# Attention and mixture-of-experts in one kernel: four new plans for the order of its steps

## The chip, the core and the metric

One NeuronCore of a Trainium2 chip runs the whole program, in one launch. The metric is the device time of that launch in microseconds (us), the median of several executions.

## What is computed

The reference pools k and v by 8 along the sequence, forms softmax attention of 8 batches with 8 heads, and sends the 4608 resulting tokens through a two-level mixture of 4 x 4 experts, where each token goes to one expert:

```
k_p, v_p = k, v averaged over 8 neighbours          # (8, 8, 72, 64)
attn     = softmax(q @ k_p.T / 8) ; attn_out = attn @ v_p
x        = attn_out as 4608 tokens of 512 numbers
g        = argmax(x @ w_group)  ; g_w = softmax weight of g
e        = argmax(x @ w_expert[g]) ; e_w = softmax weight of e
out      = g_w * e_w * (relu(x @ w1[g, e]) @ w2[g, e])
```

Everything is float32. The kernel makes the large products exact by splitting each operand into a rounded part and a rest and adding three products.

## The kernel before

The kernel works batch by batch. `Att` (L171) holds the attention and the router of one batch of 576 tokens, `Moe` (L570) the expert products of one batch, `Left` (L669) the tokens that did not choose their batch's most common expert. Three batches are in work at a time: while the expert products of batch b run, the attention of batch b+1 runs between them, and the inputs of batch b+2 are loaded and pooled.

Nothing is scheduled by a tool at run time. The order of the steps is four strings, START, FIRST, STEADY and LAST (L34 to L92), which `run` (L927) reads word by word: a word such as `n.nm:4:v` calls the method `nm` of the next batch's attention with the arguments 4 and "v". The letter ahead of the dot says whose step it is: `a` and `m` are attention and experts of batch b, `n` the attention of b+1, `w` the experts of b+1, `x` the attention of b+2, `l` the left-over tokens, `t` a warm-up or a small load. START runs once ahead of batch 0, FIRST is batch 0, STEADY is used for each of batches 1 to 6, LAST is batch 7. Each engine takes its instructions strictly in the order that these strings give it, and so do the DMA queues of SP and ACT; an instruction that waits holds up all that stand behind it on its engine.

The steps that the text speaks of, with their lines and engines:

- `kr`, `vr`, `rr` (L235, L253, L239) pool k, v and the 16 remaining rows. Their last argument picks the form: "p" three additions on Pool (L228, L229, L233), "v" the same three on DVE, "r" one reduction on DVE (L225).
- `sc`, `mx`, `sb`, `ex`, `su_`, `nm` (L328 to L376) are scores, maximum, subtraction, exponential, sum and division for one of 5 pieces of the sequence; `nm` multiplies on Pool ("p") or DVE ("v"), L373 and L376. `px_` and `pm` (L381, L400) turn the result on TensorE; `pxa`, `pma` (ACT) and `pxd`, `pmd` (DVE) split it. `av`, `ava`, `avd` (L418, L421, L425) multiply by v and split the result x.
- `kt` and `kta` (L287, L308): the pooled k turned on TensorE and taken out of PSUM by ACT. `sc` needs it.
- `xr` (L432): x put together again by eight additions on Pool; `rt` (L441) multiplies it by the router's weights, `route` (L455 to L483), `count` (L489), `main_expert`, `elect` (L496 to L508) find the batch's most common expert on DVE, and `gex`, `gates`, `keep_x` (L539 to L568) the gates.
- `w.load` (L584) loads the eight 512 KB weight slices of that expert over SP's queue, `split` (L591) rounds a slice on ACT, `spd` (L596) subtracts to get the rest, 2.4 us on Pool or 1.2 us on DVE.
- `up`, `ua`, `upd` (L609, L614, L619): first product on TensorE, relu on ACT, rest on DVE. `down`, `da` (L648, L661): second product and its output. Both use the same three PSUM buffers, so a product starts only when an earlier result was taken out.
- `l.step` (L692 to L757) builds the list of left-over tokens, `l.which` (L759) picks the first group, `l.xtiles` (L806) fills two 128 x 2304 tiles with zeros on Pool (L810).

Of the kernel before, what the change touches and what calls it, by code (L numbers as in the profile page):

```python
# [34 lines left out]
t.warm:20 a.load_v:0 a.vr:0:r a.load_k:1:w a.load_r:k a.load_k:0:w a.load_r:v t.warm:4 a.load_v:1 t.load_wr t.warm:18 a.load_q:0 a.kr:1:v a.load_q:4  # L35
a.rr:v a.kb a.load_q:1 t.warm:11 a.kr:0:p a.kt a.kta a.rcopy a.load_q:2 n.load_r:v a.vr:1:v a.guess_x a.qt:0 n.load_r:k a.guess_e a.qta:0 a.qt:1
a.qta:1 a.vmain m.load:1:1 a.sc:0 a.mx:0 a.vm:0 a.sb:0 a.ex:0 a.sc:1 a.su_:0 a.vm:1 n.load_k:1 t.warm:4 a.nm:0:v a.mx:1 a.px_:0 m.load:1:3 a.pm:0
a.pxa:0 a.vrem a.pma:0 m.load:1:2 a.sb:1 a.pxd:0 a.ex:1 a.vrx t.warm:7 a.pmd:0 t.warm:2 a.su_:1 a.av:1:0:128 a.av:0:0:128 a.ava:1:0:128 a.avd:1:0:128
a.load_q:3 a.ava:0:0:128 a.nm:1:p a.qt:2 m.load:1:0 a.avd:0:0:128 a.av:2:0:128 a.qta:2 a.av:3:0:128 a.ava:2:0:128 n.load_v:0 a.ava:3:0:128 n.load_k:0
a.avd:2:0:128 n.load_qb:0 a.sc:2 a.avd:3:0:128 n.load_qb:2 m.split:1:1 a.pm:1 a.px_:1 n.load_qb:3 a.mx:2 a.pxa:1 a.pma:1 a.sb:2 a.ex:2 m.split:1:0  # L40
m.spd:1:0:p a.pxd:1 a.qt:3 a.qta:3 a.pmd:1 t.warm:8 a.av:1:128:128 a.ava:1:128:128 a.su_:2 a.av:2:128:128 a.av:3:128:128 m.spd:1:1:p a.avd:1:128:128
n.load_qb:1 a.av:0:128:128 a.ava:2:128:128 a.ava:0:128:128 a.avd:0:128:128 a.ava:3:128:128 a.avd:3:128:128 a.sc:3 a.avd:2:128:128 m.up:0:0 m.ua:0:0
# [3 lines left out]
a.pma:2 a.mx:4 a.su_:3 m.spd:1:2:v t.warm:4 a.sb:4 m.up:4:0 m.split:1:3 a.nm:3:p a.ex:4 a.pxd:2 a.pmd:2 a.su_:4 n.vr:0 m.up:2:0 m.ua:4:0 a.pm:3
m.upd:4:0 a.nm:4:p a.px_:3 m.ua:2:0 m.upd:2:0 a.pma:3 a.pxa:3 a.px_:4 a.pxa:4 a.pmd:3 a.pxd:3 m.up:3:0 a.pm:4 a.pma:4 m.upd:1:0 a.pxd:4 a.pmd:4
m.ua:3:0 a.av:2:256:320 a.ava:2:256:320 a.avd:2:256:320 m.split:2:0 n.kr:0:r a.av:0:256:320 a.ava:0:256:320 m.upd:3:0 a.av:1:256:320 a.av:3:256:320
m.load:2:2 a.ava:3:256:320 a.ava:1:256:320 m.spd:1:3:p n.kr:1:p a.avd:3:256:320 m.up:5:0 n.rr:p m.split:2:1 m.ua:5:0 m.spd:2:1:p a.avd:1:256:320
m.spd:2:0:p a.avd:0:256:320 n.load_v:1 m.up:6:0 m.ua:6:0 m.upd:5:0 a.rt n.kt n.kta m.upd:6:0 n.qb:0 m.up:1:1 n.qb:1 a.route n.sc:0 n.mx:0 n.sb:0  # L50
n.ex:0 m.up:7:0 a.count x.load_r:v n.sc:1 m.ua:7:0 n.qb:2 n.su_:0 m.up:0:1 n.rcopy n.nm:0:p n.mx:1 m.upd:7:0 n.px_:0 m.ua:0:1 m.ua:1:1 m.up:2:1 n.sb:1
n.ex:1 m.upd:0:1 n.qb:3 x.load_k:1 n.su_:1 n.nm:1:p a.gex n.sc:2 n.pxa:0 n.mx:2 n.vrem m.upd:1:1 m.load:2:3 m.ua:2:1 m.up:4:1 n.pm:0 m.upd:2:1 n.px_:1
x.load_r:k m.ua:4:1 n.pxa:1 m.up:3:1 n.pm:1 n.sb:2 n.pxd:0 n.pma:1 m.ua:3:1 a.keep_x n.qb:4 n.vr:1:p t.warm:4 t.warm:2 n.vmain a.gates n.ex:2
# [919 lines left out]
```

## Time and profile before

| | us |
|---|---|
| three executions | 599.0, 599.31, 601.17 |
| their median | 599.31 |
| the profiled execution, on its own clock | 602.23 |
| its span, first to last instruction | 600.4 |
| TensorE busy | 573.5 |
| DVE busy | 408.2 |
| Pool busy | 303.9 |
| ACT busy | 277.6 |

The profile is one execution. In the views below a line starts with the time of its first instruction in us from the span's start and its length; in brackets stand the idle time ahead of it and what ended that. The mean granted clock of TensorE was 0.98 of full speed. Two levels are seen, 1.00 and 0.50.

### The profile page before, as it was taken

The page shows a single profiled execution, that of the slowest core. Times are in us where ns is not written, and L with a number is a line of the kernel's source. Part 1 is how long each engine was busy: PE and PEld are TensorE (multiplying, and loading weights), DVE is VectorE, ACT ScalarE, POOL GpSimd, SP SyncE. Part 2 cuts the span into 40 slices and gives each one's busy share as a digit, 9 for nine tenths or more (in the row PEclk, how much of TensorE's full clock was granted, in tenths as well). Part 3 has the DMA queues.
Part 4 walks back from the last instruction along what each step waited for, and adds up shares of the span by engine and source line. Part 5 has one row for each costly group of instructions (what it writes and reads, how often), then busy time and mean ns, then how long its engine had stood idle before and what let it go on. Part 6 is the DMA issues. An engine that isn't in the chain of part 4 may idle for free. (4 is left out here: it accounts for less than half of the span.)

```text
span 600.4 us, 13256 instructions
## 1 busy us (share of the span) xinstructions
PE 573.5 (96%) x4970; PEld 511.4 (85%) x4970; DVE 408.2 (68%) x1104; ACT 277.6 (46%) x621; POOL 303.9 (51%) x296
## 2 busy tenths in 40 slices
...
DMA packets 119362, 81.45 MB, mean 136 GB/s; under 512 B 76790, under 2 KB 95990, under 8 KB 118912
## 3 DMA queue, kind: packets, MB, share of 16 engines
...
## 5 line engine op out<-in xcount | busy, mean ns | idle before, releaser
L609 PE MATMUL mm<-xt,w 128*128 128x320 f32 (+1 forms) x1536 | 225.8, 302 | 7.4 <-DVE kT L755 4.7
L609 PEld LDWEIGHTS mm<-xt,w 128*128 128x128 f32 x1536 | 209.7, 191 | 11.3 <-DVE kT L755 4.9
L648 PE MATMUL mm<-w,ht 128*128 128x512 f32 x744 | 184.7, 400 | 0.0
L596 POOL TENSOR_TENSOR w<-sw,w 128x1024 fp32r<-128x1024 f32 x55 | 131.6, 2401 | 82.5 <-ACT w L591 69.2
L648 PEld LDWEIGHTS mm<-w,ht 128*128 128x128 f32 x744 | 139.0, 191 | 30.2 <-issue 1.8
L614 ACT ACTIVATE ht<-mm 128x320 fp32r<-128x320 f32 (+1 forms) x128 | 52.2, 410 | 76.1 <-PE mm L609 73.9
L619 DVE SCALAR_TENSOR_TENSOR ht<-mm,ht 128x256 fp32r<-128x256 f32 (+1 forms) x192 | 63.9, 367 | 28.1 <-ACT ht L614 27.7
L591 ACT CAST w<-sw 128x1024 fp32r<-128x1024 f32 x64 | 67.0, 1047 | 31.7 <-DMA sw<-in_moe_w_dram 28.4
L432 POOL TENSOR_TENSOR sw<-xt 128x256 f32<-128x256 f32 (+1 forms) x56 | 43.6, 807 | 46.9 <-DVE xt L425 46.9
L661 ACT ACTIVATE y<-mm,gm 128x512 f32<-128x512 f32 x31 | 21.3, 687 | 89.6 <-PE mm L648 88.2
L342 DVE TENSOR_REDUCE mx<-sc 128x8 f32<-128x576 f32 (+1 forms) x40 | 30.0, 751 | 41.3 <-PE sc L336 40.6
L373 POOL TENSOR_TENSOR px<-p,su 128x128 f32<-128x128 f32 (+1 forms) x38 | 17.1, 450 | 72.0 <-DVE su L365 58.1
L376 POOL TENSOR_TENSOR p<-p,su 128x576 f32<-128x576 f32 (+1 forms) x38 | 43.8, 1152 | 3.0
L358 ACT ACTIVATE p<-p 128x576 f32<-128x576 f32 (+1 forms) x40 | 27.4, 685 | 24.4 <-DVE p L353 19.9
L425 DVE TENSOR_TENSOR xt<-tp,xt 128x320 fp32r<-128x320 f32 (+2 forms) x68 | 28.8, 439 | 12.4 <-ACT xt L421 11.2
L336 PEld LDWEIGHTS sc<-kT,qT 64*64 64x64 f32 x1264 | 24.2, 137 | 14.2 <-issue 8.1
L363 DVE TENSOR_REDUCE su<-p 128x8 f32<-128x576 f32 (+1 forms) x40 | 29.9, 747 | 8.8 <-ACT p L358 8.7
L336 PE MATMUL sc<-kT,qT 64*64 64x72 f32 x1264 | 30.2, 234 | 5.2 <-ACT kT L308 2.0
L421 ACT CAST xt<-tp 128x320 fp32r<-128x320 f32 (+2 forms) x68 | 25.4, 387 | 18.8 <-PE tp L418 16.7
L653 PE MATMUL mm<-w,ht 128*128 128x512 f32 x128 | 31.8, 392 | 0.0
L353 DVE TENSOR_TENSOR p<-sc,mx 128x288 f32<-128x288 f32 x70 | 28.6, 450 | 2.8 <-POOL rp L273 0.7
L653 PEld LDWEIGHTS mm<-w,ht 128*128 128x128 f32 x128 | 24.0, 188 | 5.7 <-issue 0.6
(235 smaller groups left out, 757.4 us busy)
## 6 DMA issues: line engine op xcount, KB each, us to landing
...
```

Of the source, the lines that this page charges most:

```text
L336: nc.tensor.matmul(ps[t:t + 64, y, SP * g:SP * g + SP], lhsT=s.qT[c][r, g, t:t + 64], rhs=k, start=True, stop=True)
L342: red(out=mx[0:n], in_=scv, axis=AX.X, op=ALU.max)
L363: red(out=su[0:n], in_=s.p[c][0:n], axis=AX.X, op=ALU.add)
L376: eng.tensor_tensor(out=p[0:n], in0=p[0:n], in1=su[0:n].unsqueeze(3).broadcast_to([n, 2, 4, SP]), op=ALU.mult)
L432: nc.gpsimd.tensor_tensor(out=s.xw[g][:, sl], in0=s.xt[:, 0, g, sl].bitcast(F32), in1=s.xt[:, 1, g, sl].bitcast(F32), op=ALU.add)
L591: nc.scalar.copy(out=wh, in_=raw)
L596: (nc.vector if eng == "v" else nc.gpsimd).tensor_tensor(out=wl, in0=raw, in1=wh.bitcast(F32), op=ALU.subtract)
L609: nc.tensor.matmul(ps[:, 0:n], lhsT=l[:, kc, fs], rhs=xt[:, r, kc, sl], start=(kc == 0 and i == 0), stop=(kc == 3 and i == 2))
L614: nc.scalar.activation(out=s.ht[f][:, o:o + n], in_=s.pu[f, hf][:, 0:n], func=AF.Relu)
L619: stt(out=ht[:, at:at + hi - lo], in0=ps[:, lo - o:hi - o], scalar=0.0, in1=ht[:, lo:hi].bitcast(F32), op0=ALU.max, op1=ALU.subtract)
L648: nc.tensor.matmul(ps, lhsT=s.ht[f][:, 640 * l + o:640 * l + o + 128], rhs=s.w[2, f // 2][r][:, f % 2, :], start=(i == 0), stop=(i == 23))
L653: nc.tensor.matmul(ps, lhsT=s.ht[f][:, 512:640], rhs=s.w[2, f // 2][r][:, f % 2, :], start=(i == 0), stop=(i == 15))
```

## The change

Only the four strings are different; no function is touched, and START has one line more, so that every line number of the program is one higher. The same steps are called with the same data. What is different is their order on every engine, the number of warm-up matmuls (87 calls instead of 95), and for some steps the engine. The words that a reader needs, of some 110 changed lines:

```
 FIRST = """
-x.load_qb:2 n.av:1:0:256 n.nm:3:p n.px_:3 n.pxd:2 n.pxa:3 n.ava:1:0:256 n.mx:4 n.sb:4 n.ex:4 t.warm:1 m.spd:2:2:p x.load_qb:0 n.pxd:3 n.su_:4 n.pm:3
-n.pma:3 m.down:0 m.down:1 m.split:2:3 n.av:0:0:256 n.pmd:3 n.av:2:0:256 n.ava:0:0:256 n.nm:4:v n.avd:1:0:256 n.avd:0:0:256 n.av:3:0:256 n.ava:2:0:256
+m.upd:4:1 n.pmd:2 n.pxa:2 n.av:1:0:256 n.nm:3:p n.mx:4 n.px_:3 n.sb:4 n.ava:1:0:256 n.ex:4 n.pxd:2 n.su_:4 n.pxa:3 x.load_qb:1 n.avd:1:0:256 m.down:0
+x.load_v:0 n.nm:4:p n.pxd:3 n.pm:3 n.pma:3 m.down:1 m.split:2:3 n.pmd:3 n.av:0:0:256 m.spd:2:3:p n.ava:0:0:256 n.av:2:0:256 m.upd:7:1 n.av:3:0:256
...
 STEADY = """
-x.load_v:1 n.xr:3:256:320 m.down:0 x.kr:1:p m.down:1 x.kr:0:p n.rt m.down:2 m.da:0 m.down:6 m.down:3 n.route n.main_expert m.down:4 m.down:5 x.qb:0
-w.load:1:0 w.load:1:1 m.da:1 w.split:1:0 x.rr:v x.kt x.vr:1:v w.load:1:3 n.gex m.down:7 m.down:8 w.load:1:2 m.down:12 w.spd:1:0:p x.rcopy w.load:2:0
-x.vrem w.split:1:1 m.da:2 n.keep_x m.down:9 x.kta x.vmain w.load:2:1 x.sc:0 x.mx:0 x.sb:0 x.qb:1 n.gates x.ex:0 x.vm:0 m.down:10 m.down:13 x.su_:0
+n.av:2:0:256 n.avd:0:0:256 n.ava:2:0:256 x.kr:1:p x.load_r:k m.ua:7:1 n.xr:0:0:256 n.avd:1:0:256 n.avd:2:0:256 n.av:3:0:256 n.av:0:256:320
...
+n.avd:3:256:320 n.xr:2:256:320 n.xr:3:256:320 x.kr:0:r x.load_v:1 n.rt m.down:2 m.down:3 m.da:0 m.down:6 n.route x.qb:0 n.main_expert x.rr:r
+w.load:1:0 m.down:4 w.load:1:1 m.down:7 x.vr:1:p m.down:5 m.da:1 x.kt x.rcopy n.gex x.kta n.gates w.split:1:0 w.split:1:1 x.vrem m.down:8 w.load:2:0
+m.down:9 x.vmain w.spd:1:0:v x.sc:0 w.load:1:2 m.da:2 w.load:1:3 m.down:10 x.qb:1 x.vrx w.spd:1:1:p x.mx:0 x.sb:0 m.down:11 x.ex:0 m.down:12 m.da:3
...
 LAST = """
-l.xtiles m.upd:3:0 m.up:3:1 m.split:2:1 m.load:2:2 m.ua:4:1 l.which l.tiles m.spd:2:1:p m.upd:4:1 m.ua:3:1 m.up:5:0 m.upd:3:1 m.ua:5:0 l.fetch_x
+m.up:5:1 m.load:2:2 m.upd:3:0 l.xtiles m.split:2:1 m.upd:3:1 l.tiles m.spd:2:0:p m.up:5:0 m.ua:5:0 m.up:6:1 m.load:2:3 m.ua:5:1 m.split:2:2 l.which
```

Three places show what this does to the engines' queues. The first is ACT in STEADY, from the first outputs of batch b's second product (y) to the pooled k of batch b+2 (kT); w and sw are weight slices. Before:

```order
L661 ACTIVATE y<-mm,gm 128x512
L662 DMA out_dram<-y 128x512
L591 CAST w<-sw 128x1024
L539 ACTIVATE dg<-dg 128x20
L539 ACTIVATE de<-de 128x20
L247 DMA rp<-rp 32x128 x2
L272 CAST rh<-rp 32x128
L591 CAST w<-sw 128x1024
L661 ACTIVATE y<-mm,gm 128x512
L662 DMA out_dram<-y 128x512
L308 ACTIVATE kT<-tp 128x2x128
L309 ACTIVATE kT<-tp 128x2x16
```

And with the change:

```order
L662 ACTIVATE y<-mm,gm 128x512
L663 DMA out_dram<-y 128x512
L248 DMA rp<-rp 32x128 x2
L540 ACTIVATE dg<-dg 128x20
L540 ACTIVATE de<-de 128x20
L309 ACTIVATE kT<-tp 128x2x128
L310 ACTIVATE kT<-tp 128x2x16
L592 CAST w<-sw 128x1024 x2
L273 CAST rh<-rp 32x128
L261 CAST kp<-vp 128x256
L662 ACTIVATE y<-mm,gm 128x512
L663 DMA out_dram<-y 128x512
```

The two steps of `kta` stood behind both roundings of weight slices; now they stand ahead of them.

The second place is Pool in STEADY, around the eight additions of `xr` (sw from xt; kv, kp, vp are the pooling of k and v). Before:

```order
L373 TENSOR_TENSOR px<-p,su 128x128
L376 TENSOR_TENSOR p<-p,su 128x576
L432 TENSOR_TENSOR sw<-xt 128x256 x2
L432 TENSOR_TENSOR sw<-xt 128x320
L432 TENSOR_TENSOR sw<-xt 128x256 x2
L432 TENSOR_TENSOR sw<-xt 128x320 x3
L228 TENSOR_TENSOR kv<-kv 128x2x256
L229 TENSOR_TENSOR kv<-kv 128x2x128
L233 TENSOR_TENSOR kp<-kv 128x128
```

And with the change:

```order
L374 TENSOR_TENSOR px<-p,su 128x128
L377 TENSOR_TENSOR p<-p,su 128x576
L229 TENSOR_TENSOR kv<-kv 128x2x256
L230 TENSOR_TENSOR kv<-kv 128x2x128
L234 TENSOR_TENSOR vp<-kv 128x128
L229 TENSOR_TENSOR kv<-kv 128x2x256
L230 TENSOR_TENSOR kv<-kv 128x2x128
L234 TENSOR_TENSOR kp<-kv 128x128
L433 TENSOR_TENSOR sw<-xt 128x256 x4
L433 TENSOR_TENSOR sw<-xt 128x320 x4
```

Two poolings, of a half of v and a half of k, now run on Pool ahead of the eight additions; before, a pooling of k followed them (a second one stood behind it), and the half of v was DVE's.

The third place is DVE in LAST, where the list of left-over tokens is closed (kv, pos, kT, niti) and the first group picked (kb); ht is the rest of a first product. Before:

```order
L745 SCALAR_TENSOR_TENSOR kv<-kv,loh 128x640
L746 TENSOR_REDUCE pos<-kv 128x40
L747 TENSOR_SCALAR pos<-pos 128x40
L619 SCALAR_TENSOR_TENSOR ht<-mm,ht 128x256
L753 MEMSET it 128x1
L755 TENSOR_SCALAR kT<-cum 128x1
L756 CAST niti<-kT 128x1
L619 SCALAR_TENSOR_TENSOR ht<-mm,ht 128x256
L763 TENSOR_SCALAR kb<-cum,it 128x128
```

And with the change:

```order
L746 SCALAR_TENSOR_TENSOR kv<-kv,loh 128x640
L747 TENSOR_REDUCE pos<-kv 128x40
L748 TENSOR_SCALAR pos<-pos 128x40
L620 SCALAR_TENSOR_TENSOR ht<-mm,ht 128x256
L754 MEMSET it 128x1
L756 TENSOR_SCALAR kT<-cum 128x1
L757 CAST niti<-kT 128x1
L620 SCALAR_TENSOR_TENSOR ht<-mm,ht 128x256
L620 SCALAR_TENSOR_TENSOR ht<-mm,ht 128x64
L620 SCALAR_TENSOR_TENSOR ht<-mm,ht 128x256 x2
L620 SCALAR_TENSOR_TENSOR ht<-mm,ht 128x64
L764 TENSOR_SCALAR kb<-cum,it 128x128
```

The closing operations kept their order; the picking of the first group moved behind four more rests. On Pool, in both, a weight subtraction, the two fills of zeros and another subtraction follow one another there.

## Rows read from the trace of the kernel before

**Rows 1.** The page: busy time, share of the span and instructions of each engine.

```profile
PE 573.5 (96%) x4970; PEld 511.4 (85%) x4970; DVE 408.2 (68%) x1104; ACT 277.6 (46%) x621; POOL 303.9 (51%) x296
```

**Rows 2.** Waits of TensorE: engine, line, releaser: us in total, times, longest.

```profile
PE mm L609 <- DVE kT L755: 4.7, 1, 4.7
PE tp L418 <- DVE xt L425: 2.3, 1, 2.3
PE tp L489 <- DVE oh L483: 2.1, 2, 1.1
PE sc L336 <- ACT kT L308: 2.0, 1, 2.0
PE mm L609 <- ACT y L661: 1.8, 3, 1.2
PE sc L336 <- DVE p L349: 1.8, 1, 1.8
PE sc L336 <- DVE p L353: 1.2, 1, 1.2
```

**Rows 3.** TensorE in time: the router's product of batches 2, 3 and 7.

```profile
169.74 1.28 PE L441 MATMUL tp<-sw,wr 128*32 128x160 f32 x32
...
234.59 1.28 PE L441 MATMUL tp<-sw,wr 128*32 128x160 f32 x32
...
499.74 1.28 PE L441 MATMUL tp<-sw,wr 128*32 128x160 f32 x32
```

**Rows 4.** ACT in time, around 318 us (STEADY).

```profile
317.81 1.05 ACT L591 CAST w<-sw 128x1024 fp32r<-128x1024 f32 x1 [3.56 <-DMA sw<-in_moe_w_dram]
```

**Rows 5.** Pool, DVE and ACT in time, around 455 us (STEADY).

```profile
455.36 2.40 POOL L596 TENSOR_TENSOR w<-sw,w 128x1024 fp32r<-128x1024 f32 x1
...
455.46 2.31 DVE L549 SCALAR_TENSOR_TENSOR se<-sg,se 128x5 f32<-128x5 f32 x1
...
460.45 0.72 ACT L666 ACTIVATE y<-y,gm 64x512 f32<-64x512 f32 x1 [3.19 <-DVE y L665]
```

**Rows 6.** Pool and DVE in time, around 95 us (FIRST).

```profile
94.05 2.38 POOL L596 TENSOR_TENSOR w<-sw,w 128x1024 fp32r<-128x1024 f32 x1 [1.62 <-ACT w L591]
...
94.42 2.15 DVE L373 TENSOR_TENSOR px<-p,su 128x128 f32<-128x128 f32 x1
```

**Rows 7.** Two stretches behind it: length, PE, PEld, DVE, ACT, POOL busy, PEclk, DMA.

```profile
99.00:100.00 1.00, 1.00 (x4) 0.81 (x3) 0.84 (x4) 0.79 (x4) 0.70 (x2) 0.50 0.00 0
102.00:103.00 1.00, 1.00 (x7) 0.91 (x6) 0.26 (x1) 0.00 (x0) 0.00 (x0) 0.79 0.00 0
```

**Rows 8.** Pool, DVE and TensorE in time, around 540 us (LAST).

```profile
537.11 2.39 POOL L596 TENSOR_TENSOR w<-sw,w 128x1024 fp32r<-128x1024 f32 x1 [10.05 <-PE mm L609]
...
541.39 2.02 POOL L810 MEMSET pl<- 128x2304 f32 x1
...
537.37 6.08 DVE L747 TENSOR_SCALAR pos<-pos 128x40 f32<-128x40 f32 x1
...
524.26 14.60 PE L609 MATMUL mm<-xt,w 128*128 128x256 f32 x108
543.53 11.14 PE L609 MATMUL mm<-xt,w 128*128 128x320 f32 x60 [4.66 <-DVE kT L755]
```

**Rows 9.** Pool in time, around `xr` of batch 3 (STEADY).

```profile
228.28 0.74 POOL L432 TENSOR_TENSOR sw<-xt 128x256 f32<-128x256 f32 x1 [6.55 <-DVE xt L425]
...
234.88 1.30 POOL L228 TENSOR_TENSOR kv<-kv 128x512 f32<-128x512 f32 x1
236.26 0.74 POOL L229 TENSOR_TENSOR kv<-kv 128x256 f32<-128x256 f32 x1
237.08 0.50 POOL L233 TENSOR_TENSOR kp<-kv 128x128 f32<-128x128 f32 x1
```

**Rows 10.** DVE: its wait for the router's product, and a pooling as one reduction.

```profile
DVE lg L459 <- PE tp L441: 24.7, 7, 3.6
...
L225 DVE TENSOR_REDUCE kp<-kv 128x128 f32<-128x1024 f32 x1 | 2.0, 2031 | 0.0
```

More of the change, by code (lines that the diff above doesn't have):

```diff
@@ L34 @@
 START = """
[L35 to L42, printed above, removed]
+t.warm:21 t.load_wr a.load_k:0:w a.load_v:0 a.load_k:1:w a.load_r:k t.warm:18 a.load_r:v a.load_v:1 a.kr:0:v a.vr:0:r t.warm:4 t.warm:10 a.load_q:0
@@ new lines @@
+a.rr:v a.load_q:1 a.kr:1:p a.kb a.kt a.kta a.vr:1:v a.rcopy n.load_r:v a.load_q:2 a.guess_x a.qt:0 n.load_r:k a.guess_e a.vmain a.qt:1 a.vrem a.qta:0
+a.qta:1 a.sc:0 a.sc:1 a.mx:0 t.warm:4 a.vm:0 a.sb:0 a.ex:0 a.su_:0 n.load_k:1 a.vm:1 m.load:1:1 a.nm:0:p a.px_:0 a.load_q:3 a.vrx m.load:1:3
+m.load:1:2 a.qt:2 a.pxa:0 a.pm:0 a.mx:1 a.sb:1 a.pma:0 t.warm:7 a.pxd:0 a.ex:1 a.pmd:0 a.av:1:0:128 a.av:0:0:128 a.su_:1 a.qta:2 a.ava:1:0:128
+a.ava:0:0:128 a.avd:1:0:128 a.av:2:0:128 a.ava:2:0:128 m.load:1:0 a.nm:1:p a.av:3:0:128 a.ava:3:0:128 a.avd:0:0:128 a.load_q:4 n.load_k:0 a.sc:2
@@ L46 @@
[L46 to L53, printed above, removed]
@@ L62 @@
-x.kta m.down:9 m.down:7 x.sc:0 w.split:1:0 w.load:1:2 x.qb:1 x.mx:0 x.sb:0 w.load:1:3 x.vrem x.ex:0 w.load:1:1 w.load:2:1 m.down:8 n.gates x.su_:0
-w.spd:1:0:v m.da:2 w.split:1:1 x.nm:0:p m.down:12 x.vr:1:p m.down:13 m.da:4 x.vr:0:p m.down:10 m.down:11 m.da:3 w.spd:1:1:p x.vmain x.vm:1 w.load:2:0
-x.vrx n.keep_x x.vm:0
+m.ua:0:0 m.up:1:0 m.load:2:1 a.nm:2:p a.qt:4 m.ua:1:0 a.mx:3 a.sb:3 t.warm:2 m.upd:0:0 a.ex:3 a.pm:2 a.qta:4 a.px_:2 a.su_:3 a.sc:4 n.vr:0 a.mx:4
+t.warm:7 m.split:1:2 m.spd:1:2:v a.pma:2 m.up:4:0 a.nm:3:p a.sb:4 a.pxa:2 a.ex:4 m.up:2:0 a.pmd:2 a.pm:3 m.ua:4:0 a.px_:3 a.su_:4 m.ua:2:0 m.up:3:0
@@ new lines @@
+n.xr:0:0:256 n.pma:4 n.xr:3:0:256 n.pmd:4 n.av:0:256:320 n.av:1:256:320 x.kr:0:r n.ava:0:256:320 n.ava:1:256:320 n.avd:0:256:320 n.av:3:256:320
+n.avd:1:256:320 n.av:2:256:320 n.xr:0:256:320 n.ava:3:256:320 n.avd:3:256:320 n.xr:1:256:320 n.ava:2:256:320 m.down:3 n.xr:3:256:320 x.qb:0
+n.avd:2:256:320 n.xr:2:256:320 x.rr:r m.da:0 m.upd:6:1 m.down:4 n.rt x.kr:1:p m.down:5 n.route x.kt m.down:6 n.main_expert x.qb:1 m.da:1 m.down:7
+x.kta n.gex x.rcopy x.sc:0 x.mx:0 w.load:1:0 m.down:12 x.vrem x.sb:0 w.split:1:0 w.load:1:3 x.vrx x.ex:0 x.su_:0 m.down:8 w.spd:1:0:v w.load:1:1
```

61 lines of the change are left out of this document (35 added, 26 removed).

## The prediction, made before the change was run
> **What bounds the kernel now.** I read the page's busy times first, then TensorE's list of waits, then the five places that this list names, in order of time on all engines. The busy times show one engine that is hardly ever free: TensorE works 573.5 of 600.4 us [rows 1], so 26.9 us is all that any new order can win from gaps, and DVE, ACT and Pool matter only where TensorE waits for them. The list of waits says where: 4.7 us in LAST behind DVE's L755; in FIRST 2.3 us behind DVE's L425, 2.1 us behind L483 and 1.2 us behind L353; in STEADY 2.0 us behind ACT's L308 and 1.8 us behind ACT's L661; in START 1.8 us behind L349 [rows 2]. They add up to 15.9 us; the rest of the idle time is the launch, the end, and pieces of some tenths.
>
> What stands behind these waits is to be seen on two engines. In FIRST, Pool begins a weight subtraction of 2.38 us at 94.05, and DVE's small L373, which begins at 94.42, takes 2.15 us: it ends about when Pool's does [rows 6]. In STEADY, L549, five numbers per partition, takes 2.31 us beside a Pool operation of 2.40 [rows 5], and ACT then waits 3.19 us for DVE's y. In LAST, L747 takes 6.08 us beside a Pool queue of 2.39 us and two fills of 2.02 us each [rows 8]. So a small DVE operation between two SBUF tiles that comes just behind a Pool operation stands until Pool is done, and all of DVE's queue behind it: the evictions that free PSUM too. The wait for L308 is of another kind: ACT stood 3.56 us at a weight slice that had not landed [rows 4], with the eviction of kT queued behind it.
>
> A gap also costs afterwards. Behind the gap of 2.3 us in FIRST the granted clock is 0.50 from 99 on and 0.79 in 102 to 103 [rows 7], the lower of the two levels (1.2 and 2.4 GHz) for some 3.8 us, in which TensorE does what 1.9 us do at full clock. In LAST the 108 matmuls ahead of the gap took 14.60 us, 0.135 each; the 60 behind it took 11.14 where that rate gives 8.1, so 3.0 us more [rows 8].
>
> **The change, part by part.** TensorE's products are the same; eight of 95 warm-up calls go, but these stand where TensorE waits anyway, so I give them no term.
>
> FIRST: `nm` of piece 4 goes from DVE to Pool. L373 is then on Pool's own queue and cannot stand against it, and the evictions behind it (L425) come on time: 2.3 us of gap and 1.9 us of clock. The router's steps meet less Pool work, because the poolings of k stand elsewhere: the 2.1 us and 1.2 us can go. Ends: 0 and -7.5 us. I take -5, since the first 4.2 us have one clear cause and the other 3.3 us depend on Pool's new order.
>
> STEADY: the five intervals between the router's products of batches 2 and 7 last 499.74 - 169.74 = 330.0 us, the shortest 234.59 - 169.74 = 64.85 [rows 3]. Had all been like it, they would have taken 324.25: 5.75 us is lost to unlucky batches. The new order puts `kta` ahead of both roundings, so a late slice no longer holds the eviction of kT; and `gates` goes ahead of `sc` of the next batch, and with it L549 ahead of that Pool subtraction. Ends: 0 and -5.75; I take -5, because both named causes are gone by position. Three operations are added to DVE or changed there. `kr:0` and `rr` become reductions of 2.03 us [rows 10], the first where DVE waits 24.7 / 7 = 3.5 us per batch for the router's product [rows 10], the second behind `main_expert`, with no one waiting but the copy of rp; if that cover went, a batch would pay up to 2 us. The weight subtraction that goes to DVE stands in the same idle stretch. Loads on SP keep their number; k:0 goes ahead of the second slices, which wait for buffers anyway. The two poolings put on Pool ahead of `xr` take 2 x (1.30 + 0.74 + 0.50) = 5.1 us; Pool stood idle there for 6.55 us [rows 9], so they cost nothing with 1.5 us to spare.
>
> LAST: 7.7 us hang on L747 (4.7 of gap, 3.0 of clock). The order of the closing operations stays, and on Pool subtraction, fill, fill, subtraction still follow one another. The subtraction waits for the rounding of slice 1:3 (1.05 us, as in rows 4), the rounding for the relu of the same product whose rest DVE takes just ahead of L755. So the same matmul releases both, DVE has to bring its small operation through in about 1 us, and it has three operations of the list to finish first. Before, it missed by 0.26 us (537.37 against 537.11) [rows 8]. L747 itself stands two places earlier than L755 and should get through; L755 may well be caught. The Trainium skill, "SBUF — State Buffer", section "Who interferes with whom", says that the shared port pair is an exclusive lock for one whole instruction, and that the second to come waits until the first is finished; by that a caught L755 would go on after Pool's 2.4 us, before TensorE needs the buffer behind it, and the whole 7.7 us would be won. The row speaks against that here: L747 was not let in between the subtraction and the fills, but only after all three. By the row a caught L755 stands some 6 us, TensorE meets a full PSUM about 3 us later, and with the clock 5 to 6 of the 7.7 us come back. The picking of the first group (L763) then stands beside the next subtractions and can cost 1 to 2 us more. Ends: 0 and -7.7; I take -2, by the nearest row, L747.
>
> START: `nm:0` goes from DVE to Pool, a `kr` and `vr` change places. The four weight slices that end this stretch are asked for by the same chain, so I take 0; the ends are its one wait, 1.8 us, either way.
>
> New waits: hand-written places that are moved get gaps of their own; of the kind of L489, about 1.0 us each [rows 2]. I take two, +2 us; ends 0 and +4.
>
> Sum: -5 - 5 - 2 + 0 + 2 = -10 us. The profiled execution took 602.23, so 592.2. It lies 2.9 us above the median of the runs shown, 599.31; part of that may be the late slice at 318, if other executions do not have it, and the new order would not feel it. So I set no part of the 2.9 against the sum: **592 us**, 7 us below the median.
>
> **Rivals.**
> 1. The lock is handed over between Pool instructions, or L755 comes in time, and LAST gives all 7.7 us: 592.2 - 5.7 = 586.5 us. For it: DVE stood beside one Pool operation alone in its 2.31 us [rows 5]. Against it: the 6.08 us of L747 [rows 8]. It is what the page of the Trainium skill named above states as its rule.
> 2. Nothing is won in sum. The small operations are as many as before (DVE loses only the extra steps of pooling), every Pool operation is still there, and what is taken from one neighbour gets another: five waits of some 2 us come back elsewhere, about 599 us. For it: the best interval has no slack to give. Against it: the two STEADY causes vanish by order alone.
> 3. Slower. Pool's additions for `xr` now wait for a half of k that SP loads late in the batch, behind the q pieces, on the only engine that `rt` waits for. The cover is 1.5 us of Pool time. If the load, or `nm:4` ahead of it, is 4 us late, each of six STEADY batches loses 2.5 us at `rt`: 592 + 15 = 607 us. It decides from 1.7 us beyond the cover on, where 6 x 1.7 eats the 10 us. For it: DVE waits behind `rt`, and Pool's last addition ends within tenths of it. Against it: SP issues that load behind twelve of the sixteen q pieces, not at the end, and it needs no buffer that Pool has yet to free.
>
> **How the numbers follow.** Forecast 0.45, rival 1 0.22, rival 2 0.20, rival 3 0.13. A measurement of this kernel can tell 0.5%, 3.0 us, from no change, so "same" is 596.3 to 602.3. Forecast, rival 1 and a little of rival 2 lie below: faster 0.68. Most of rival 2: same 0.20. Rival 3: slower 0.12. The range goes from 584, which leaves out the case in which every end comes at its best (602.2 - 7.5 - 5.75 - 7.7 = 581.3), up to 601, which leaves out rival 3.
>
> **What would show it.** Right: TensorE's list of waits has no L308 and no L661 above a few tenths, the five intervals between router products all lie near 65 us, and in FIRST no gap of 2 us is left behind L425. L549 takes a fraction of a microsecond in most batches. In LAST, the length of L755 (L756 in the new numbering) tells forecast from rival 1: 2 us or less, or 4 to 6 us with a gap on TensorE behind it. Wrong: a wait of `rt` (L441, L442 in the new numbering) for Pool in every batch is rival 3; new waits of 2 us at names that the list does not have now are rival 2.

## Result and profile after

The changed kernel takes **578.14 us** (median of 4 runs, 577.8 to 578.97) against 599.61 in the runs beside it: a ratio of 0.964, 95% interval 0.9619 to 0.9662. The forecast was 592.0, the range 584 to 601. The direction was right; the gain is 21.5 us where 7 against the median were forecast, and the time lies 6 us below the range. (Line numbers after are one higher than before, L756 is what L755 was.)

The page's busy times of the change, then the head of TensorE's list of waits (us in total, times, longest):

```profile
PE 562.8 (98%) x4954; PEld 504.6 (88%) x4954; DVE 392.1 (68%) x1072; ACT 273.9 (48%) x621; POOL 305.8 (53%) x304
```
```profile
PE sc L337 <- DVE p L350: 1.7, 1, 1.7
PE mm L922 <- DVE valid L127: 1.1, 1, 1.1
PE tp L419 <- ACT ph L406: 0.7, 1, 0.7
```

Of [rows 2] only the wait in START is left at its size. TensorE's idle time went from 26.9 to 13.7 us. But its busy time fell as well, by 10.7 us [rows 1], with the same products and eight warm-up calls fewer: a part of what it was "busy" with was waiting, too. The mean granted clock of TensorE rose from 0.980 to 0.992; of the two levels 1.00 and 0.50 that is, as an estimate, some 24 us at the lower one before and 9 after.

The router's product of batches 2, 3 and 7 in time (answers to [rows 3]):

```profile
160.40 1.28 PE L442 MATMUL tp<-sw,wr 128*32 128x160 f32 x32
...
225.01 1.28 PE L442 MATMUL tp<-sw,wr 128*32 128x160 f32 x32
...
483.47 1.28 PE L442 MATMUL tp<-sw,wr 128*32 128x160 f32 x32
```

Read as stages, these products and the spans say where the time came from:

| stretch | before, us | after, us | difference |
|---|---|---|---|
| start to the router's product of batch 1 | 108.57 | 101.29 | -7.3 |
| from there to batch 2's | 61.17 | 59.11 | -2.1 |
| five STEADY intervals | 330.00 | 323.07 | -6.9 |
| from batch 7's to the end | 100.66 | 93.02 | -7.6 |
| span | 600.4 | 576.5 | -23.9 |

The five intervals are 64.59 to 64.65, without one gap of TensorE above 0.2 us. The two STEADY causes are gone. L550 takes 0.17 us in all eight batches; before, L549 took 2.31 in two of eight, one of them the batch of [rows 5]. DVE in time, in that batch:

```profile
434.87 0.17 DVE L550 SCALAR_TENSOR_TENSOR se<-sg,se 128x5 f32<-128x5 f32 x1
```

And ACT hardly stands at weight slices any more: both waits that are left lie in FIRST, the longer one up to 113.9 us. Its wait for them, from the list of waits of before and then of after (total, times, longest):

```profile
ACT w L591 <- DMA sw<-in_moe_w_dram: 28.4, 17, 3.6
```
```profile
ACT w L592 <- DMA sw<-in_moe_w_dram: 6.9, 2, 6.5
```

In FIRST the stretch from 95 to 103 us, in which [rows 6, 7] showed a gap and the lower clock, is full, and the granted clock stays at its upper level (columns as in [rows 7]):

```profile
95.00:103.00 8.00, 8.00 (x67) 6.59 (x66) 6.70 (x11) 2.30 (x5) 7.12 (x9) 1.00 0.28 98
```

In LAST, DVE and Pool at the place of [rows 8]:

```profile
520.42 0.18 DVE L748 TENSOR_SCALAR pos<-pos 128x40 f32<-128x40 f32 x1
520.86 0.15 DVE L756 TENSOR_SCALAR kT<-cum 128x1 f32<-128x1 f32 x1
525.12 1.91 DVE L764 TENSOR_SCALAR kb<-cum,it 128x128 f32<-128x128 f32 x1
...
520.62 2.41 POOL L597 TENSOR_TENSOR w<-sw,w 128x1024 fp32r<-128x1024 f32 x1 [12.30 <-ACT w L592]
522.97 2.02 POOL L811 MEMSET ph<- 128x2304 f32 x1
524.93 2.02 POOL L811 MEMSET pl<- 128x2304 f32 x1
526.91 2.42 POOL L597 TENSOR_TENSOR w<-sw,w 128x1024 fp32r<-128x1024 f32 x1
```

L748 begins 0.20 us ahead of Pool's subtraction, where before it began 0.26 us behind; it takes 0.18 us where L747 took 6.08. And L756, one number per partition, takes 0.15 us in the middle of Pool's subtraction: it was not held at all. These tenths are no luck of one execution. In all nine traces with the new LAST up to there (the change, e1, e6, e8, e10, e11, e13, e14, e18 below), L748 begins 0.19 to 0.20 us ahead of Pool and takes 0.18; in all nine with before's LAST (before, e2, e3, e5, e9, e12, e15, e16, e17), L747 begins 0.26 to 0.27 behind and takes 6.07 or 6.08.

### The profile page after: what moved, and what is told of

Same layout as the page of the kernel before. It is cut to its first block, busy times and chain, and to the rows that moved or that the text cites. A ratio compares the mean times of both kernels' runs of the same rounds, so it can differ in the third digit from the quotient of the medians.

```text
span 576.5 us, 13216 instructions
## 1 busy us (share of the span) xinstructions
PE 562.8 (98%) x4954; PEld 504.6 (88%) x4954; DVE 392.1 (68%) x1072; ACT 273.9 (48%) x621; POOL 305.8 (53%) x304
## 5 line engine op out<-in xcount | busy, mean ns | idle before, releaser
L610 PE MATMUL mm<-xt,w 128*128 128x320 f32 (+1 forms) x1536 | 220.4, 300 | 0.1
L649 PE MATMUL mm<-w,ht 128*128 128x512 f32 x744 | 179.9, 395 | 0.0
L649 PEld LDWEIGHTS mm<-w,ht 128*128 128x128 f32 x744 | 136.9, 188 | 29.5 <-issue 1.8
L597 POOL TENSOR_TENSOR w<-sw,w 128x1024 fp32r<-128x1024 f32 x47 | 114.1, 2444 | 35.6 <-ACT w L592 35.6
L615 ACT ACTIVATE ht<-mm 128x320 fp32r<-128x320 f32 (+1 forms) x128 | 50.2, 411 | 63.3 <-PE mm L610 62.1
L620 DVE SCALAR_TENSOR_TENSOR ht<-mm,ht 128x256 fp32r<-128x256 f32 (+1 forms) x192 | 60.0, 348 | 23.3 <-ACT ht L615 22.5
L662 ACT ACTIVATE y<-mm,gm 128x512 f32<-128x512 f32 x31 | 21.2, 684 | 106.3 <-PE mm L649 106.3
L274 POOL TENSOR_TENSOR rp<-rp,rh 32x128 f32<-32x128 f32 x8 | 3.6, 455 | 94.1 <-DMA rp<-rp 92.0
L374 POOL TENSOR_TENSOR px<-p,su 128x128 f32<-128x128 f32 (+1 forms) x40 | 17.2, 429 | 62.7 <-DVE su L366 54.2
L377 POOL TENSOR_TENSOR p<-p,su 128x576 f32<-128x576 f32 (+1 forms) x40 | 46.1, 1152 | 3.1
L426 DVE TENSOR_TENSOR xt<-tp,xt 128x320 fp32r<-128x320 f32 (+2 forms) x68 | 28.5, 437 | 13.7 <-ACT xt L422 12.6
L337 PEld LDWEIGHTS sc<-kT,qT 64*64 64x64 f32 x1264 | 24.0, 136 | 10.7 <-issue 6.8
L229 POOL TENSOR_TENSOR kv<-kv 128x512 f32<-128x512 f32 x21 | 33.0, 1570 | 0.2
L654 PE MATMUL mm<-w,ht 128*128 128x512 f32 x128 | 30.9, 391 | 0.0
```

The costliest lines, as they stand in the source:

```text
L229: add(out=a[:, :, 0:256], in0=a[:, :, 0:256], in1=a[:, :, 256:512], op=ALU.add)
L337: nc.tensor.matmul(ps[t:t + 64, y, SP * g:SP * g + SP], lhsT=s.qT[c][r, g, t:t + 64], rhs=k, start=True, stop=True)
L377: eng.tensor_tensor(out=p[0:n], in0=p[0:n], in1=su[0:n].unsqueeze(3).broadcast_to([n, 2, 4, SP]), op=ALU.mult)
L597: (nc.vector if eng == "v" else nc.gpsimd).tensor_tensor(out=wl, in0=raw, in1=wh.bitcast(F32), op=ALU.subtract)
L610: nc.tensor.matmul(ps[:, 0:n], lhsT=l[:, kc, fs], rhs=xt[:, r, kc, sl], start=(kc == 0 and i == 0), stop=(kc == 3 and i == 2))
L615: nc.scalar.activation(out=s.ht[f][:, o:o + n], in_=s.pu[f, hf][:, 0:n], func=AF.Relu)
```

## Experiments

Medians, with the 95% interval of the ratio to the kernel before:

| run | what | us | interval |
|---|---|---|---|
| e1_last | before, LAST of the change | 592.07 | 0.9852 to 0.990 |
| e2_steady | before, STEADY of the change | 595.82 | 0.9917 to 0.9959 |
| e3_first | before, START and FIRST of the change | 587.97 | 0.9769 to 0.9834 |
| e4_fills | before, fills one place later | 600.12 | 0.9991 to 1.0029 |
| e7_step | change, one eviction ahead of two steps | 584.15 | 0.9713 to 0.9763 |
| e5_nm4 | before, `nm:4` on Pool | 598.77 | 0.997 to 1.0007 |
| e6_nm4back | change, `nm:4` on DVE | 579.44 | 0.9651 to 0.9683 |
| e12_nm4_spd | e5 and a subtraction on DVE | 601.10 | 1.0014 to 1.0058 |
| e15_first_letters | before, FIRST's engines alone | 597.95 | 0.9969 to 1.0017 |
| e16_vr_ahead | e5 and three places | 598.55 | 0.9966 to 1.0 |
| e17_vr_only | before, three places | 600.90 | 1.0003 to 1.0043 |
| e18_vr_behind | change, poolings of v put back | 581.63 | 0.9666 to 0.9717 |
| e10_letters | change, STEADY's engines as before | 587.29 | 0.9744 to 0.9809 |
| e13_spd_letter | change, one of them as before | 581.91 | 0.969 to 0.9753 |
| e14_pool_letters | change, the other four as before | 583.31 | 0.9714 to 0.9776 |
| e8_nowarm | change, FIRST without warm-up calls | 579.31 | 0.9616 to 0.9667 |
| e9_warm8 | before, eight warm-up calls fewer | 598.61 | 0.9957 to 0.9997 |
| e11_slots | change, last group's preparation earlier | 577.80 | 0.9597 to 0.9644 |

### Which plan gave what

```diff
 # e1_last, e2_steady, e3_first: open the kernel before, replace
-LAST = before's      (e1)    -STEADY = before's   (e2)    -START, FIRST = before's   (e3)
+LAST = the change's  (e1)    +STEADY = the change's (e2)  +START, FIRST = the change's (e3)
```

> The kernel before, with the plan LAST alone taken from the change. Theory 1, the three parts do not lean on each other and the traces price each: from the last router product to the end 100.7 us went to 93.0, so this run should stand 7 to 8 us below the kernel before, at about 592 us; in its trace L748 (the subtraction on the positions) takes 0.2 us, begun ahead of Pool's weight subtraction, and TensorE has no wait of 4.7 us there. Theory 2, what LAST gained hangs on the state in which STEADY leaves the engines (which instruction of DVE meets which of Pool by a few tenths of a microsecond): L748 is caught again, 597 to 600 us.

> The kernel before, with the plan STEADY alone taken from the change. Theory 1: the five intervals between router products go from 330.0 to about 323.1 us, all within 0.1 us of 64.6, so 7 us less than the profiled execution of before; as that one lay 2.6 us above the median, which may be the late weight slice in one of its batches, the run itself should show 4.5 to 7 us, 592.5 to 595 us. Theory 2, the loads and the new order need the FIRST plan that fills the buffers for them: the intervals stay uneven, and the time lies above 597 us.

> The kernel before, with the plans START and FIRST taken from the change (they belong together, one step stands in the other). Theory 1: the second router product stands 9.3 us earlier in the trace of the change (160.40 against 169.74), and nothing behind it gives that back, so about 590 us. Theory 2, what is won ahead is lost later, because STEADY's weight slices then land later against the work that needs them: 593 to 599 us, with waits behind the roundings of slices (L308 or L592) in the list.

Measured: LAST -1.2%, STEADY -0.6%, START and FIRST -2.0%. The three ratios multiply to 0.962, the change's is 0.964 (0.9619 to 0.9662): no sign that the parts lean on each other, which is theory 1 each time, with STEADY a little below its size and FIRST above. START and FIRST give most, 11.9 us (by the interval 10 to 14); the trace of e3 locates 8.9 of them, since its router's product of batch 2 comes at 160.89. STEADY gives 3.7, less than the two traces say: in nine other traces with before's STEADY (e1, e3, e4, e5, e9, e12, e15, e16, e17) the five intervals take 325.9 to 330.3 us, 327.0 in the mean, so the 330.0 of the profiled execution was an unlucky one. With the new plan (e2) they are 64.59 to 64.65 each.

### What a Pool row does to a small DVE operation (LAST)

```diff
 # e4_fills, in LAST of the kernel before
-m.up:5:1 l.xtiles m.upd:3:0 ... m.spd:2:1:p m.upd:4:1
+m.up:5:1 m.upd:3:0 ... m.spd:2:1:p l.xtiles m.upd:4:1
 # e7_step, in LAST of the change
-m.ua:4:1 l.step m.upd:4:0 l.step m.spd:1:3
+m.ua:4:1 m.upd:4:0 l.step l.step m.spd:1:3
```

> The kernel before, with one step of LAST moved: the two fills of zeros stand behind Pool's second weight subtraction instead of ahead of it. Theory 1, a DVE operation that Pool's subtraction has caught goes on when that subtraction ends, if another subtraction comes next, and only fills let it wait on: L747 takes about 2.2 us instead of 6.08, TensorE's wait of 4.7 us behind L755 shrinks to 1 us or none, and with the clock kept the time is 593 to 595 us. Theory 2, it waits until Pool's queue has a pause, whatever stands in it: L747 takes about 8 us (four Pool operations), and the time is 600 to 602 us. Theory 3, by the exclusive lock for one instruction that the Trainium skill states (SBUF - State Buffer, Who interferes with whom) the fills never mattered as such: L747 would be let in behind the first subtraction here, as in theory 1, but it would have been in the kernel before too, where the trace shows 6.08 us.

> The change, with one eviction in LAST (m.upd:4:0) put ahead of the two closing steps instead of between them, so that DVE reaches L748 (128x40, from SBUF to SBUF) about a microsecond later, when Pool's subtraction has begun. Theory 1, the gain of LAST hangs on these tenths: L748 is caught until both fills are done, 5 to 6 us, TensorE waits some 4 us behind the evictions, and the clock falls behind it: 583 to 586 us. Theory 2, the lock passes on behind each Pool instruction: L748 takes about 2 us, no TensorE wait above 1 us, 578 to 579 us.

DVE and Pool of e4_fills in time:

```profile
536.35 2.17 DVE L747 TENSOR_SCALAR pos<-pos 128x40 f32<-128x40 f32 x1
538.78 0.14 DVE L755 TENSOR_SCALAR kT<-cum 128x1 f32<-128x1 f32 x1
539.36 5.47 DVE L763 TENSOR_SCALAR kb<-cum,it 128x128 f32<-128x128 f32 x1
...
536.09 4.75 POOL L596 TENSOR_TENSOR w<-sw,w 128x1024 fp32r<-128x1024 f32 x2 [10.25 <-PE mm L609]
540.77 2.02 POOL L810 MEMSET ph<- 128x2304 f32 x1
542.73 2.02 POOL L810 MEMSET pl<- 128x2304 f32 x1
```

L747 is let in at the seam of two subtractions after 2.17 us, as theory 1 says; the next one, L763, is caught by the second subtraction and now it stands through both fills, 5.47 us. The evictions queue behind it, and TensorE waits nearly as long as before:

```profile
PE mm L609 <- DVE ht L619: 5.7, 4, 3.9
```

The victim changed, the price hardly, and so the time is the same: the mechanism of theory 1 is right and its time was wrong, since I had not looked at who comes next. DVE and Pool of e7_step in time, then TensorE's longest wait:

```profile
521.83 5.34 DVE L748 TENSOR_SCALAR pos<-pos 128x40 f32<-128x40 f32 x1
...
520.78 2.44 POOL L597 TENSOR_TENSOR w<-sw,w 128x1024 fp32r<-128x1024 f32 x1 [12.30 <-ACT w L592]
523.16 2.02 POOL L811 MEMSET ph<- 128x2304 f32 x1
525.11 2.02 POOL L811 MEMSET pl<- 128x2304 f32 x1
527.10 4.68 POOL L597 TENSOR_TENSOR w<-sw,w 128x1024 fp32r<-128x1024 f32 x2
```
```profile
PE mm L610 <- DVE ht L620: 3.7, 1, 3.7
```

One eviction's place puts L748 a microsecond behind Pool's start, and 6.0 of LAST's 7.4 us are gone: theory 1. L748 goes on when the second fill gives way to a subtraction. The granted clock is 0.75 from 525 to 530 and 0.91 from 530 to 535.

### The named cause in FIRST, and the poolings of v

```diff
 # e5_nm4, in FIRST of the kernel before          # e6_nm4back, in FIRST of the change
-n.nm:4:v                                         -n.nm:4:p
+n.nm:4:p                                         +n.nm:4:v
 # e12_nm4_spd: e5, and w.spd:1:1:p -> w.spd:1:1:v
 # e15_first_letters: e5, e12 and m.spd:1:3:v x.kr:0:r x.rr:r
 # e17_vr_only (e16_vr_ahead: with e5's edit)
-x.sc:0 w.split:1:0 ... x.vrem x.ex:0 ... n.gates x.su_:0 ... x.nm:0:p m.down:12 x.vr:1:p m.down:13 m.da:4 x.vr:0:p ... w.spd:1:1:p x.vmain
+x.sc:0 x.vrem w.split:1:0 ... x.ex:0 ... x.su_:0 ... x.vr:1:p x.vr:0:p x.nm:0:p m.down:12 m.down:13 m.da:4 ... w.spd:1:1:p n.gates x.vmain
 # e18_vr_behind, in FIRST of the change
-x.vr:0:p m.da:2 x.vr:1:p m.down:13 ... x.nm:0:p w.spd:1:1:v
+m.da:2 m.down:13 ... x.nm:0:p x.vr:0:p x.vr:1:p w.spd:1:1:v
```

> The kernel before, with one engine changed: the last scaling by 1/sum of the second batch in FIRST (L373 and the product behind it) goes from DVE to Pool. Theory 1, the prediction's: the wait of 2.3 us behind L425 and the 1.9 us of lower clock behind it go, 595 to 596 us. Theory 2: the evictions that TensorE waits for then wait for Pool's queue instead, and the gap stays, 599 to 600 us.

> The change, with that one operation in FIRST put back from Pool to DVE. Theory 1: it meets Pool's weight subtraction again, a gap of about 2 us and the lower clock behind it come back, 581 to 582.5 us. Theory 2, it was the place that mattered, not the engine: in the new order Pool runs no long operation there, and the time stays within 1 us of the change, 577.5 to 579 us.

> The kernel before, with two engine changes in FIRST: the scaling nm:4 goes to Pool, and the weight subtraction w.spd:1:1, which stands in Pool's unbroken row 12 us later, goes to DVE. Theory 1: the scaling alone gave back what it won because Pool then ran without a pause from 124.9 to 138 and TensorE met a wait of 2.0 us there; with one subtraction of 2.4 us off Pool that wait goes below 0.7 us, the second router product comes 2 to 3 us earlier than before (167 to 168), and the time is 596 to 597 us. Theory 2: Pool is not what bounds that stretch; 598.5 to 600 us, as with the scaling alone.

> The kernel before, with all five engine changes of FIRST and none of its moves. Theory 1: what FIRST gains is the relief of Pool and of DVE's small operations by the engines alone; the second router product comes at 161 to 163, 590 to 592 us. Theory 2: the order is needed as well, since the waits ahead of the first product of the second layer (4 us there) hang on where the evictions and the warm-up calls stand; the second router product comes at 165 to 168, 594 to 597 us. Theory 3: without the moves the engines gain nothing, 598 to 600 us.

> The kernel before, with the scaling nm:4 of FIRST on Pool and, behind the router's product of the second batch, three steps placed as the change has them: the rounding of the remainder (x.vrem) ahead of the rounding of a weight slice that has yet to land, the two poolings of v (5.3 us of Pool) ahead of the first scaling instead of behind it, the gate's arithmetic behind the scaling. Theory 1: the gain of nm:4 was lost because ACT stands at that slice, Pool begins the scaling late, and the rounding of v on ACT, with the relus behind it, waits for the poolings that follow; with the poolings done during ACT's wait, TensorE's wait of 2 us at 136 goes below 0.7, the second router product comes at 166 to 168, and the time is 596 to 597 us. Theory 2: the slice's landing alone sets that stretch; the second router product stays at 170, 598.5 to 600 us.

> The same three places, with nm:4 left on DVE. Theory 1: the places alone win only the 0.6 us that TensorE waits there in the kernel before; second router product near 169, 598.5 to 599.5 us, so that the two together win more than each alone. Theory 2: the places cost something of their own; 600 us or more.

> The change, with the two poolings of v in FIRST (5.3 us of Pool) put back behind the first scaling of the batch, as the kernel before has them. Theory 1: ACT's rounding of v then waits for them with the relus behind it, TensorE waits some 2 us more around 125, the second router product comes at 162 to 163 instead of 160.4, and the time is 580 to 581.5 us. Theory 2: in the new order the place of these poolings does not matter; within 1 us of the change, 577.5 to 579 us.

Up to the router's product of batch 1, e5, e12 and e16 run the same program; it comes at 107.23, 106.00 and 105.58, where before, e1, e2, e4 and e17 have 108.57, 108.51, 108.54, 109.79 and 110.48. The means differ by 2.9 us, and the stretch from the second layer's first product (L648) on shows the same without scatter: 17.95 to 18.00 us in those five traces, 15.09 in each of the three. So the scaling on Pool does win what TensorE lost there, two thirds of the 4.2 us. But the next interval, 61.17 before, is then 62.78, 64.23 and 62.74, and nothing is left in the time. In e12, which theory 1 expected to cure this, the interval is the longest: Pool's row of subtractions is not what bounds it, and that theory fell.

The trace of e5 shows ACT at its rounding of v behind Pool's poolings, with the relus that free PSUM behind it. The wait of 1.98 us itself ends on DVE: the addition to su, eight numbers per partition, was held beside a Pool subtraction, and the rest of a first product (L619), on which TensorE waits, queued behind it. DVE in e5:

```profile
135.64 1.66 DVE L364 TENSOR_SCALAR su<-su 128x8 f32<-128x8 f32 x1
```

In e12 and e16 the same operation takes 0.17 us and the loss stays, so this hold is not what decides. In e12 ACT stands 3.19 us at that rounding, and TensorE's wait is 2.90. Moving the poolings ahead in the kernel before (e16) did take that wait away, but TensorE waits there almost as long as in e5, 1.86 us in two pieces against 1.98: now ACT's scalings of v and of the remainder, 2.2 us, stand in a row ahead of the relu. How much of the loss each row causes was not taken apart. Alone (e17) the three places cost 1.4 us in that interval. Theory 1 fell for e16 and e17: the times are those of theory 2, though in e16 batch 2's product comes at 168.32 and not at 170. In the change, the same place counts. ACT's rounding of v in time and TensorE's longest wait, both in e18_vr_behind, then the same rounding in the change:

```profile
125.98 0.41 ACT L261 CAST kp<-vp 128x256 fp32r<-128x256 f32 x1 [4.48 <-POOL vp L234]
```
```profile
PE mm L610 <- DVE ht L620: 2.0, 1, 2.0
```
```profile
122.13 0.41 ACT L261 CAST kp<-vp 128x256 fp32r<-128x256 f32 x1 [0.42 <-ACT y L662]
```

With the poolings behind the scaling the interval is 62.90 instead of 59.11 and the time 3.5 us longer (3.1 by the two ratios): theory 1, both a little above its figures, with batch 2's product at 163.82. So FIRST's gain has two halves that need each other: the products ahead come earlier, and the stretch behind does not give that back. With all five engine changes and no move (e15) the router's products come at 105.61 and 168.59, and the time does not differ from before: theory 3. In the change the scaling put back on DVE (e6) costs 1.3 us by the medians, at the edge of what the two intervals tell apart; its trace has 0.8 us more behind the second layer's first product (15.69 against 14.9). It begins at 89.83, takes 0.28 us, and Pool's subtraction begins only at 90.64. There the place had made it nearly harmless already (theory 2, though the time lies 0.4 us above its range).

Batch 1's product comes 8.0 us earlier with the change (mean of eight traces with the change's FIRST up to there, 101.2, against 109.2). Of these, 3.1 lie behind the second layer's first product (14.9 us against 18.0), which the scaling alone nearly gives, and 4.5 ahead of it: from the first layer's first product on it takes 47.8 us in all eight, against 51.9 to 53.1 before. (The other 0.4 lie ahead of both products, where single traces differ by up to 1.8.) FIRST's engines alone (e15, 51.3) do not give these 4.5, nor do fewer warm-up calls (e9 below, 53.1), so they need the moves. Which of them was not taken apart.

### STEADY: order or engines

```diff
 # in STEADY of the change
-x.vr:0:p ... x.kr:0:r ... x.rr:r ... x.vr:1:p ... w.spd:1:0:v
+x.vr:0:v ... x.kr:0:p ... x.rr:v ... x.vr:1:v ... w.spd:1:0:p     # e10: all, e13: w.spd alone, e14: the first four
```

> The change, with its STEADY order kept and the five changes of engine or form in it taken back: the poolings x.vr:0 and x.vr:1 on DVE and x.kr:0 on Pool and x.rr on DVE by additions, one weight subtraction on Pool, as before. Theory 1, the order alone makes the six intervals even, and the reductions of 2 us were only free: intervals of 64.6 to 65 us, 578 to 580 us. Theory 2, the engine is what counts, since DVE's additions of pooling stand between SBUF tiles and meet Pool's work while a reduction does not: the intervals go back to 65 us and more with waits behind DVE, 581 to 586 us. Theory 3, kr:0 on Pool stands ahead of nothing that waits, but the additions of rr hold DVE ahead of the mover of q: one wait of about 1 us per batch, 584 us.

> The change, with one letter of STEADY taken back: the weight subtraction w.spd:1:0 on Pool as before. Theory 1: this letter is the one of the five that counted, because on Pool two subtractions of 2.4 us follow one another just ahead of the first scaling of the next batch; intervals of 66 to 66.8 us, 585 to 588 us. Theory 2: the loss of 9 us came from the poolings; 578 to 580 us.

> The change, with the other four letters of STEADY taken back (the poolings and the sum of the remainder on the engines and in the form of before), the weight subtraction left on DVE. Theory 1: these are free where they stand; intervals of 64.6 to 65 us, 578 to 579.5 us. Theory 2: DVE's additions of pooling meet Pool's work and hold DVE; 580 us or more.

Against the change, e10 loses 9.1 us, e13 3.8 and e14 5.2 by the medians (8.2, 4.9 and 6.3 by the ratios): both halves count, and in the traces they nearly add up, 8.7, 3.5 and 5.9 us from batch 1's router product to batch 7's. For e13 each theory held a part; for e14 the time is theory 2's. STEADY's order alone is worse than before's STEADY: e10 loses more than the 3.7 us that STEADY gives (e2), and its five intervals take 330.6 us against 327.0 in the mean above. What it lacks is not the named causes, which stay away in e10 (no wait behind L309 or L662, L550 at 0.17 in every batch); two other waits come in their place, 2.7 us behind Pool's L374 and 3.7 behind DVE's L394, the first as in e13, the second as in e14. TensorE's longest wait in e13, Pool there in one of these batches, then Pool in the change:

```profile
PE tp L382 <- POOL px L374: 2.9, 4, 1.2
```
```profile
181.32 4.77 POOL L597 TENSOR_TENSOR w<-sw,w 128x1024 fp32r<-128x1024 f32 x2
186.04 0.40 POOL L374 TENSOR_TENSOR px<-p,su 128x128 f32<-128x128 f32 x1
```
```profile
181.21 2.41 POOL L597 TENSOR_TENSOR w<-sw,w 128x1024 fp32r<-128x1024 f32 x1
184.03 0.41 POOL L374 TENSOR_TENSOR px<-p,su 128x128 f32<-128x128 f32 x1 [0.41 <-DVE su L366]
```

With two subtractions in a row the first scaling of the next batch starts 2.0 us later, and TensorE waits for it. In e14 the wait is another one, for DVE:

```profile
PE tp L419 <- DVE pr L394: 4.1, 5, 1.2
```
```profile
282.75 0.68 DVE L229 TENSOR_TENSOR kv<-kv 128x512 f32<-128x512 f32 x1
283.47 0.43 DVE L230 TENSOR_TENSOR kv<-kv 128x256 f32<-128x256 f32 x1
283.93 0.29 DVE L234 TENSOR_TENSOR vp<-kv 128x128 f32<-128x128 f32 x1
284.25 0.44 DVE L394 TENSOR_TENSOR pr<-tp,pr 32x64 fp32r<-32x64 f32 x2
```

The three additions of a pooling of v, 1.4 us, stand on DVE ahead of the rest that TensorE waits for, in each of the five batches. In three of the five they take their usual time to 0.05 us (0.69, 0.43 and 0.29), and TensorE waits 0.6 to 0.7 us all the same: it is their place in DVE's row that costs. That Pool holds them, which theory 2 had as the reason, is not what the trace shows in these three.

### Warm-up calls and the end

```diff
 # e8_nowarm, FIRST of the change: t.warm:2 t.warm:7 t.warm:2 t.warm:1 t.warm:4 left out
 # e9_warm8, FIRST of the kernel before: t.warm:10 -> t.warm:2
 # e11_slots, LAST of the change
-l.hback l.fetch_a l.down m.half:3:1 l.slots l.fetch_b
+l.hback l.slots l.fetch_a l.down m.half:3:1 l.fetch_b
```

> The change, without the five groups of warm-up calls (16 calls) that its plan FIRST holds; they compute nothing that is used. In its trace they take 4.8 us of TensorE. Theory 1, as the prediction had it (they stand where TensorE waits anyway): the waits show instead, the time is that of the change, 577.5 to 579 us, or up to 2 us longer where the granted clock falls behind the longer waits. Theory 2, the new order leaves no wait there, and every call stands on the path: 4 to 5 us less, 573.5 to 574.5 us.

> The kernel before, with eight warm-up calls fewer in FIRST (one group of ten cut to two), as many fewer as the change has. The eight take about 1 us in the trace (20 records in 2.50 us). Theory 1, the prediction's: they fill a wait, and the time stays at 599 to 600 us. Theory 2, they stand on the path and explain a part of what FIRST gained beyond the two waits: 598.5 us or less.

> The change, with the last preparation of a group (l.slots, 2.7 us of small DVE operations that stand behind TensorE's last product) moved ahead of that product, where DVE is idle. Theory 1, the end of the program is DVE's chain (TensorE ends at 569.7, DVE at 572.9, the span at 576.5): 2.5 us less, 575.5 to 576 us. Theory 2, the end is set by the store of the last output and the test that ends the loop: no change, 577.5 to 578.5 us.

e8: theory 1, with the ratio of the change (0.9641 against 0.964). The two stretches 38 to 90 and 90 to 101 us of e8, then of the change (length, then PE busy and its matmuls):

```profile
38.00:90.00 52.00, 46.41 (x554) 42.13 (x545) 45.67 (x123) 29.83 (x76) 34.38 (x35) 1.00 0.52 122
90.00:101.00 11.00, 10.76 (x67) 8.98 (x69) 9.96 (x19) 4.42 (x13) 10.57 (x11) 1.00 0.45 129
```
```profile
38.00:90.00 52.00, 49.87 (x606) 46.04 (x603) 45.31 (x123) 29.84 (x76) 34.48 (x34) 1.00 0.53 124
90.00:101.00 11.00, 10.76 (x61) 9.16 (x59) 9.94 (x19) 4.87 (x13) 10.41 (x11) 1.00 0.36 120
```

Over both stretches TensorE is busy 3.5 us less, and the router's product comes within 0.5 us of the same time (100.79): the calls are waiting time that counts as work. e9 lies 0.2% below before, at the edge of what its interval tells, but batch 2's product (169.82) is not earlier, so its trace shows nothing won where the calls went; where the 0.2% comes from stays open. e11 moves 2.7 us of DVE's last chain away and gains nothing that its interval tells from the change: theory 2. None of these beats the change.

## Why the prediction was wrong, step by step

- **"26.9 us is all that any new order can win from gaps"**: the step that failed first, because the ends rest on such gaps: with every term at its best they gave 581.3 us, or 579.5 with START's 1.8, which that sum leaves out, and 578.1 was measured. The span fell by 23.9 us, with 13.7 us of idle time still there. Busy time held waits of its own: warm-up calls that fill them (e8), matmuls at the lower clock (some 24 us of it before, 9 after), and short stalls between matmuls that count as busy: in e1, whose STEADY is before's, the five intervals run at full clock with 324.6 us busy, in the change the same 2792 matmuls take 323.1. From the first product of the first layer to that of the second, the kernel before has 3.8 us of gaps and 5.7 us of warm-up calls, the change 2.1 and 4.8.
- **FIRST, -5, ends 0 and -7.5**: measured -11.9 together with START (e3; START itself, by its last step, the first product of the first layer at 38.66 and 38.51, gives 0 as forecast). This is the term that was mis-sized most. It summed three waits of the list and one stretch at the lower clock, and left out the 4.5 us that the moves win ahead of the second layer's first product, a stretch in which the list has little more than L489 and L353. And "the first 4.2 us have one clear cause" did not hold by itself: that cause removed alone wins 2.9 us and loses them by the next router product (e5).
- **LAST, -2, "by the nearest row, L747"**: measured -7.4 (e1), near the end -7.7. (Of these 7.7 the clock's part was 2.7 and not 3.0: the 108 matmuls ahead of the gap have 48 of the wider form, 128x320, the 60 behind it 36, so that the earlier rate per column gives 8.4 us and not 8.1.) The mechanism was right, its victim wrong: I expected L755 (now L756) to be caught, but an operation on one number per partition was held in neither trace, and in before L755 only queued behind L747. What decided was L748, which came 0.20 us ahead of Pool. So rival 1's price for this part was right, by its second wording (the operation comes in time) and not by a handover: behind a subtraction the fills do hold an operation for 5 to 6 us (e4, e7), and the new order escapes that by tenths, the same tenths in nine traces. The -2 lay between the two outcomes and was neither's price.
- **STEADY, -5**: measured -3.7 (e2), within its ends, and 6.9 in the profiled pair. The signs I asked for all came: no L308 and no L661, even intervals, L549 at 0.17. The first and the last say less than I thought: four of the traces with before's STEADY (e1, e9, e12, e15) have no wait behind L308 either, and L549 was short in most batches before. "Gone by position" was right, as the two causes stay away with the order alone (e10). What was wrong is the price of nothing for the engine changes: without them the same order meets two new waits and loses 9.1 us.
- **New waits, +2**: none came in STEADY or LAST, and in FIRST none above some tenths. TensorE has no gap over 0.2 us from 93 to 507 us.
- **The base**: I set nothing of the 2.9 us between the profiled execution and the median against the sum. The late slice at 318 is in e16 again (2.2 us) and in e4, e5 and e17 smaller (0.9 to 1.1), so it is a matter of the execution. Against the mean of 327.0 us for before's five intervals, the new ones had 3.9 us to win, not 5.75, which is about what e2 measured.
- **Rival 3**, the poolings ahead of the eight additions: TensorE had no gap ahead of `rt` in any batch. Rival 2 did not happen either: the small operations are as many, but most of them no longer meet Pool. In before some 24 DVE operations (L747 not counted) were held for about 26 us beyond their usual time, in the change some 19 for about 12, and 4.4 of that is L764, L782 and an addition in LAST, with no gap of TensorE behind them.
